# Keeping the bias of rows 0 to 127 on chip for six heads: a change to an attention and MLP kernel

## The chip, the cores and the metric

The kernel runs on one core of one Trainium2 chip. The metric is the device time of one execution in microseconds (us), the median of several runs.

## The reference

Attention with a bias that depends on the row i and the distance to column j, then a feed-forward block and a gated block, all in float32 on inputs of 4 batches, 8 heads, 576 rows, head width 64. Only the first part matters here:

```
def _attn_ref(q, k, v, w1, b1, w2):
    scores = scale * np.matmul(q, k.transpose(0, 1, 3, 2))
    pos = np.arange(S)
    rel = (pos[:, None] - pos[None, :]).astype(np.float32)
    x = (np.log1p(np.abs(rel)) / np.log1p(np.maximum(pos[:, None], 1.0)))[..., None]
    h = np.maximum(x @ w1 + b1, 0.0)          # 32 hidden units
    bias = h @ w2                             # 576 x 576 x 8 heads
    scores = scores + bias.transpose(2, 0, 1)[None]
    ...
```

A softmax over each row and the product with v follow; then a LayerNorm with a relu MLP and a residual; then a gated MLP and a residual.

## The kernel before, in words

**Bias stage (the first 53 us or so).** The 576 rows of the bias are made in 36 groups of 16 rows, numbered z, in the order `ORDER` (line 58): 16 to 23, 8 to 15, 0 to 7, 24 to 35. The place in that order is y, so that z = 0 is y = 16 and z = 7 is y = 23. For a group, `units` (L324) makes four tiles m (relu of a shifted log row) on ScalarE or VectorE as the table `WHO` says (L333, L335); `sums` (L338) multiplies them by w2 on TensorE into PSUM tiles pt (L347), from a pool of six; `finish` (L380) evacuates pt, scaled, into an SBUF tile o, its columns to the right and to the left of the diagonal apart, each by ScalarE (L354) or VectorE (L356) as the table `EV` says, and stores that tile. Partition 8r + h of o holds row r of the group for head h, 591 columns wide, so one tile holds all eight heads of 16 rows. The pool of m has 14 buffers, that of o (`bs`) has 10. Each loop step y issues the m tiles of y + 2, then the sums of y, then `finish` of y - 1, so each engine's order is fixed by this loop.

**The way through DRAM.** `store` (L358, the issue is L368) writes o to a scratch tensor scr in DRAM, which turns eight heads on partitions into rows on partitions when it is read back. Groups with z < FULL = 24 store all of o at once (295.5 KB), on the SP queue. Groups 24 to 35 go into three wider tiles of four groups each (the pool `aspare`, 4*591 columns); in the bias stage only heads 0 and 1 of them are stored, in two pieces for each four groups (`GROUPS`: three groups at once, 110.8 KB for a head, then the fourth, 36.9 KB; the last ones for head 1 are issued by ScalarE). The other six heads follow with a store of the whole tile (1182 KB), put into a list `held` and issued at the attention slots `HELD` = 2, 3 and 9.

**Reading back.** `read(k)` (L370) loads bias rows 128k to 128k + 127 of heads 0 and 1 (L376 for odd k; two loads for even k, L262 and L263, which turn the columns; L276 for the last 64 rows). The table `READ` says behind which y each is issued on the SP queue. The other six heads are loaded pair by pair, during the attention of the pair ahead (`load_bias`, from slot 19 on for the first of them), into two buffers `bias` that alternate, of the pools `abias0` and `abias1`.

**What else the SP queue carries there.** The raw k, q and v of the first two units (L216, L210), and `place_q` (L236), which moves halves of q between partitions.

**Attention (about 53 to 315 us).** 16 units (head pair, batch), each of 9 slots of 64 or 128 rows; a hand-written list (`FIRST` for unit 0, `SEQ` for the others) gives the order of steps: `S n` are the score products on TensorE (L708), `add n` adds the bias and takes the row minimum on VectorE (`ct`, L714), `exp n` is on ScalarE (L728), `T n` are transposes (L734). `emit_slot` (L880) issues the held stores and, for later units, the loads of q, k and v; GpSimd splits them into high and low parts (L114, L120). The two MLP blocks follow to the end.

**Completion of transfers.** The built program gives each DMA the next of eight completion semaphores, DMAHW0 to DMAHW7, in turn, and a DMA's issue first waits until the semaphore's last user has landed. An instruction that must wait for a DMA waits for its semaphore.

Of the kernel before, what the change touches and what calls it, by code (L numbers as in the profile page):

```python
# [9 lines left out]
F32 = mybir.dt.float32  # L10
# [8 lines left out]
B, H, S, D, DM = 4, 8, 576, 64, 512  # L19
# [57 lines left out]
    AA AA AA AA AA AA AA AA AD DD AA DA  # L77
""".split()

READ = {20: [2], 27: [0], 29: [1], 32: [3], 35: [4]}  # L80

FULL = 24
GROUPS = ((3, 2), (1, 3))
HELD = (2, 3, 9)
QK = 5, 16, 11, 22
GATE = 35
STAGES = 8
# [8 lines left out]
def mark(label):  # L96
    pass
# [3 lines left out]
def block_kernel(  # L101
# [8 lines left out]
    def new_pool(name, bufs, stack=None, **kw):  # L110
        return (stack or ctx).enter_context(tc.tile_pool(name=name, bufs=bufs, reuse_waits="tile", **kw))
# [82 lines left out]
    bp1 = new_pool("abias1", 1, left)  # L194
    raw, ops, bias, M = {}, {}, {}, {}
# [4 lines left out]
    M["held_at"] = right.enter_context(ExitStack())  # L200
    M["spare"] = new_pool("aspare", (36 - FULL) // 4, M["held_at"], side="right")
    Qb = [qp.tile([128, 2 * S + 64], F32R, name=f"q{j}") for j in range(2)]
# [4 lines left out]
    def load_q(u, pool_=rawp):  # L207
        hp, b = UNITS[u]
        t = raw.setdefault(u, {})["q"] = pool_.tile([128, 2, S], F32R, name="q")
        sp.dma_start(out=t[:, 1].bitcast(F32), in_=a["q"][b, hp])  # L210
# [20 lines left out]
    def place_q(u):  # L231

        t, Q = raw[u].pop("q"), Qb[u % 2]
        for h in range(2):
            for z in range(2):
                sp.dma_start(out=Q[64 * z:64 * z + 64, q_of(h)].bitcast(F32), in_=t[64 * h:64 * h + 64, z].bitcast(F32))  # L236
# [15 lines left out]
    def new_bias(hp):  # L252
        bias[hp] = (bp0, bp1)[hp % 2].tile([128, 9, S], F32, name="bias")
# [11 lines left out]
    def load_bias(hp, z):  # L265

        if hp not in bias:
            new_bias(hp)
        if z < 2:
            t = bias[hp][:, 5 * z:5 * z + 4]  # L270
            src = rows(2 * hp, 0, 512)[:, z].rearrange("(n p) j -> p n j", p=128)
            turned(t[:, ::2], src[:, ::2])
            sp.dma_start(out=t[:, 1::2], in_=src[:, 1::2])
        else:
            for h in range(2):
                sp.dma_start(out=bias[hp][64 * h:64 * h + 64, 4], in_=rows(2 * hp, 512, 64)[:, h])  # L276
# [4 lines left out]
    with ExitStack() as c:  # L281
# [32 lines left out]
        )  # L314
        pool.memset(mhalf, -0.5)
        new_bias(0)
        for t in Qb:
            pool.memset(t[:, S:S + 64].bitcast(F32), 0.0)
        def reach(z):

            l, r = 16 * z + 15, S - 16 * z
            return l, r, max(l + 1, r)
# [28 lines left out]
        def scaled(who, z, o, i):  # L351
            f = scl[:, z:z + 1]
            if who == "A":
                act.activation(o, i, AF.Copy, scale=f)  # L354
            else:
                dve.tensor_scalar(out=o, in0=i, scalar1=f, scalar2=None, op0=ALU.mult)  # L356

        def store(z, n, src, heads=None):  # L358

            f = 16 + 16 * z * H * PITCH - reach(z)[0]  # L360
            if heads is None:
                dims, src = [[PITCH, 128]], src
            else:
                f += heads * PITCH
                dims, src = [[H * PITCH, 16]], src[heads::H]
            dims += [[16 * (H * PITCH - 1), n], [1, 591]]
            q = act if heads == 1 and z + n > 34 else sp
            q.dma_start(out=bass.AP(scr.tensor, scr.offset + f, dims), in_=src.rearrange("p (s j) -> p s j", s=n))  # L368

        def read(k):  # L370
            if k == 4:
                load_bias(0, 2)
                return
            t, src = bias[0][:, k::5], rows(0, 128 * k, 128)
            if k % 2:
                sp.dma_start(out=t, in_=src)  # L376
            else:
                turned(t, src)

        def finish(z, pts):  # L380
            l, r, n = reach(z)
            if z < FULL:
                t = stg.tile([128, 591], F32, name="o")
            else:
                if z % 4 == 0:
                    spare[z // 4] = M["spare"].tile([128, 4 * 591], F32, name="o")
                t = spare[z // 4][:, 591 * (z % 4):][:, :591]
            left, right = t[:, :l + 1][:, ::-1], t[:, l:]
            for o, pt in pts:
                scaled(EV[ORDER.index(z)][0], z, (right if z < 18 else left)[:, o], pt)  # L390
            if z < 18:
                scaled(EV[ORDER.index(z)][1], z, left[:, 1:], pts[0][1][:, 1:l + 1])
            else:
                scaled(EV[ORDER.index(z)][1], z, right[:, 1:], pts[0][1][:, 1:r])
            if z < FULL:
                store(z, 1, t)
            else:

                for n, at in GROUPS:
                    if z % 4 == at:  # L400
                        for h in range(2):
                            store(z + 1 - n, n, spare[z // 4][:, 591 * (at + 1 - n):591 * (at + 1)], h)
                if z % 4 == 3:
                    M.setdefault("held", []).append(lambda: store(z - 3, 4, spare[z // 4]))
            for k in READ.get(ORDER.index(z), ()):
                read(k)

        spare = {}
# [3 lines left out]
        for y, z in enumerate(ORDER):  # L412
# [5 lines left out]
            if y >= BEHIND:  # L418
                finish(*late.pop(0))
# [12 lines left out]
            if y == QK[2]:  # L432

                KH, KL = (qkp.tile([128, 2, S + 64], F32R, name=n) for n in ("kh", "kl"))
                k = raw[0].pop("k")
# [9 lines left out]
                split_v(0)  # L445
        while late:
            finish(*late.pop(0))


    tiles = [[4 * b + j for j in range(4)] for b in range(B)] + [[16, 17]]  # L450
# [95 lines left out]
    side = {}  # L546
# [6 lines left out]
    def conv_first(rcp):  # L553

        at = [(0, 1)] + [(u, j) for u in range(1, 12) for j in range(2)]

        def put(p, f):
            conv_at.setdefault(p, []).append(f)

        for z in range(4):  # L560

            def load_piece(z=z):
                r = rcp.tile([128, 1024], I32, name="r")
                if z < 2:
                    sp.dma_start(out=r.rearrange("p (k f) -> p k f", k=2), in_=w1v[:, 2 * z:2 * z + 2, :512])
                else:
                    sp.dma_start(out=r, in_=w2v[:, z - 2])
                return r

            ld, stages, w = convert(rcp, 512, load_piece)  # L570
            i = 5 * z + 3
            put(at[i - 2], ld)
            for q, f in enumerate(stages[:5]):
                put(at[min(i + q, 22)], f)
            last = at[min(i + 4, 22)][0], 2
            put(last, stages[5])
            put(last, lambda z=z, w=w: sp.dma_start(out=wc0[z // 2, :, 512 * (z % 2):512 * (z % 2) + 512], in_=w()))
# [81 lines left out]
    with ExitStack() as c:  # L659
# [220 lines left out]
        def emit_slot(u, n):  # L880

            mark(f"att {u}.{n}")
            k = 9 * u + n
            PT[:] = PA[(k + 1) % 2], PA[k % 2]
            hp, b = UNITS[u]
            if n == 0 and u + 1 < NU:
                place_q(u + 1)
            if n == 1 and "last" in M:
                M.pop("last")()
            if n == 5 and u + 2 < NU:  # L890
                load_q(u + 2)
                load_k(u + 2)
            for f in side.pop(k - 1, []) + ([M["held"].pop(0)] if k in HELD else []):
                f()
            if k == HELD[-1]:
                M["held_at"].close()
                conv_first(new_pool("arc", 2, M["rc"]))
            if u == 12 and n == 0:
                open_first()
            if hp < 3 and b == 2 and n in (1, 4, 7):  # L900
                load_bias(hp + 1, n // 3)

        emit = dict(
            slot=emit_slot, sq=emit_sq, kh=emit_kh, vh=emit_vh, C=emit_C, cp=lambda u: emit_C(u, 2), S=emit_S, add=emit_add, exp=emit_exp, T=emit_T, hi=emit_hi, lo=emit_lo, RT=emit_RT, RThi=emit_RThi,
            RTlo=emit_RTlo, PV=emit_PV, Pev=emit_Pev, O=emit_O, Oev=emit_Oev, fo=emit_fo, fx=emit_fx, Or=emit_Or, oc=emit_oc, ra=emit_ra, rb=emit_rb, xr=emit_xr,
        )
# [511 lines left out]
def build(tc, nc, aps, out):  # L1418
    a = {n: (p.bitcast(I32) if n in ("moe_w_ch1", "moe_w_ch2", "moe2_w_in", "moe2_w_out") else p) for n, p in aps.items()}
    with tc.manual_schedule():  # L1420
        block_kernel(tc, nc, a, out)
# [18 lines left out]
```

## Time and profile before

| | |
|---|---|
| median of 3 runs | 946.3 us (946.25 to 948.57) |
| the profiled execution | 945.16 us; span of its records 943.4 us |
| TensorE busy | 922.5 us, 98% of the span |
| VectorE busy | 720.6 us, 76% |
| ScalarE busy | 494.9 us, 52% |
| GpSimd busy | 425.1 us, 45% |
| granted TensorE clock | full speed (9 of 9 tenths shown) in all 40 slices of the page |

Shares are averages over stages with different limits. Busy time is what an engine spent on instructions; a time in brackets behind a row is the idle time of the engine ahead of it, with what ended it. "L354" is line 354 of the kernel. SPq and ACTq are the queues on which SP and ScalarE issue DMAs. A DMA's landing is counted from its issue.

### The profile page before, as it was taken

The numbers are of one execution on the slowest core, as the hardware profiler recorded it, in microseconds if no ns is written. First come the engines' busy times: TensorE is split into PE (matmuls) and PEld (weight loads), VectorE is DVE, ScalarE is ACT, GpSimd is POOL, SyncE is SP. The second block draws the span as 40 slices with busy tenths as digits, with TensorE's granted clock in tenths as the row PEclk, the third lists the DMA queues.
The fourth block names the chain that finished last, engine by engine and source line by source line (L and its number), as shares of the span: only waits on it lengthen the run. The fifth ranks groups of instructions, "written<-read, shape, count | busy, mean of one in ns | idle before, by whom it ended". The sixth has DMA issues, their size and how long they took to land.

```text
span 943.4 us, 16015 instructions
## 1 busy us (share of the span) xinstructions
PE 922.5 (98%) x5681; PEld 805.8 (85%) x5681; DVE 720.6 (76%) x1433; ACT 494.9 (52%) x1108; POOL 425.1 (45%) x555
## 2 busy tenths in 40 slices
PE   7889999999999999999999999999999999999998
PEld 2269999999999888888888888888888998989996
DVE  7988999999889687885779798979765656455452
ACT  8979999999998754322222222223132635253340
POOL 0068788978999543332224333433300524133251
PEclk9999999999999999999999999999999999999999
DMA  6878847757563561212122333233222000001001
GB/s 230 283 234 258 270 137 214 236 162 226 158 206 85 177 196 31 70 33 89 61 68 92 123 99 122 88 124 99 101 67 104 23 1 23 24 0 58 1 34 67
DMA packets 57983, 110.23 MB, mean 117 GB/s; under 512 B 10032, under 2 KB 21040, under 8 KB 57648
## 3 DMA queue, kind: packets, MB, share of 16 engines
q1 hardware_dynamic: 57504, 108.64, 36.1%
q8 instruction: 45, 0.74, 0.3%
q10 hardware_dynamic: 400, 0.58, 0.2%
q14 instruction: 34, 0.28, 0.1%
HBM read 71.37 MB, written 28.38 MB: 106 GB/s over the span
## 4 chain that ended last, share of the span: by engine, by line
PE 91%; DVE 5%; POOL 1%; DMA 1%; issue 1%; ACT 1%; DVEq 0%; SPq 0%; POOLq 0%; ACTq 0%
PE psh L124 21%; PE psy L124 21%; PE psa L124 10%; PE s L708 8%; PE PB L797 8%; PE psa L1284 6%; PE pt L734 6%; PE psa L1266 5%; DVE m L335 4%; PE pt L487 1%; PE OB L803 1%; PE s L744 1%; PE pt L347 1%; DVE ct L714 0%; DMA L<-in_c_log_dram 0%
## 5 line engine op out<-in xcount | busy, mean ns | idle before, releaser
L124 PE MATMUL psh<-blk,w1h 128*128 128x512 f32 (+1 forms) x640 | 151.5, 368 | 0.0
L176 POOL TENSOR_TENSOR cvl<-cvl,cvt 128x512 f32<-128x512 f32 x44 | 56.9, 1293 | 206.6 <-DVE cvt L173 179.0
L655 ACT ACTIVATE hh<-psh 128x512 fp32r<-128x512 f32 (+1 forms) x80 | 44.1, 553 | 194.4 <-PE psh L124 193.2
L124 PEld LDWEIGHTS psh<-blk,w1h 128*128 128x128 f32 x640 | 113.3, 188 | 20.8 <-DVE blk L120 0.2
L714 DVE CUSTOM_DVE_ANT_0 ct<-s,bias 128x576 f32<-128x576 f32 x144 | 107.0, 752 | 16.6 <-PE s L708 7.1
L728 ACT ACTIVATE a<-ct,sm 128x576 f32<-128x576 f32 x144 | 112.2, 779 | 3.2 <-DVE sm L714 2.6
L1087 DVE TENSOR_TENSOR x_sb<-psy,x_sb 128x512 f32<-128x512 f32 x144 | 97.2, 683 | 9.1 <-PE psy L124 8.6
L656 DVE SCALAR_TENSOR_TENSOR hl<-psh,hh 128x512 fp32r<-128x512 f32 (+1 forms) x80 | 50.5, 632 | 56.5 <-ACT hh L655 56.5
L124 PE MATMUL psy<-w2h,hh 128*128 128x512 f32 x288 | 90.2, 394 | 0.1
L124 PE MATMUL psy<-w2l,hh 128*128 128x512 f32 x288 | 88.9, 390 | 0.0
L124 PE MATMUL psy<-w2h,hl 128*128 128x512 f32 x288 | 88.8, 389 | 0.0
L734 PE MATMUL pt<-ident,a 128*128 128x128 f32 x576 | 84.9, 273 | 0.3 <-DVE at0l L120 0.3
L124 PE MATMUL psh<-blk,w1l 128*128 128x512 f32 (+1 forms) x320 | 79.0, 368 | 0.0
L708 PE MATMUL s<-kh,q 128*128 128x288 f32 x320 | 72.0, 314 | 3.1 <-DVE sm L714 2.4
L734 PEld LDWEIGHTS pt<-ident,a 128*128 128x128 f32 x576 | 68.6, 141 | 1.1 <-DVE at0l L120 0.6
L708 PE MATMUL s<-kl,q 128*128 128x288 f32 x320 | 65.8, 295 | 0.0
L124 PEld LDWEIGHTS psh<-blk,w1l 128*128 128x128 f32 x320 | 56.8, 189 | 10.0
L124 PEld LDWEIGHTS psy<-w2l,hh 128*128 128x128 f32 x288 | 54.0, 188 | 11.5
L124 PEld LDWEIGHTS psy<-w2h,hl 128*128 128x128 f32 x288 | 54.0, 188 | 11.5
L177 POOL TENSOR_TENSOR cvw<-cvl,cvw 128x512 f32<-128x512 f32 x44 | 59.9, 1362 | 3.5
L124 PEld LDWEIGHTS psy<-w2h,hh 128*128 128x128 f32 x288 | 52.6, 188 | 9.9 <-issue 0.2
L120 DVE TENSOR_TENSOR at0l<-pt,at0h 128x512 fp32r<-128x512 f32 (+1 forms) x80 | 49.5, 619 | 5.6 <-ACT at0h L117 5.2
(202 smaller groups left out, 2173.5 us busy)
## 6 DMA issues: line engine op xcount, KB each, us to landing
r<-in_moe_w_ch_dram SPq DMA_DIRECT2D x32, 512.0 KB, 4.8
k<-in_k_dram SPq DMA_DIRECT2D x16, 640.0 KB, 5.4
q<-q SPq DMA_DIRECT2D x64, 144.0 KB, 2.7
scr<-o SPq DMA_DIRECT2D x24, 295.5 KB, 3.3
v<-in_v_dram SPq DMA_DIRECT2D x16, 384.0 KB, 3.5
q<-in_q_dram SPq DMA_DIRECT2D x16, 288.0 KB, 3.7
bias<-scr SPq DMA_DIRECT2D x8, 576.0 KB, 5.7
bias<-scr SPq DMA_DIRECT2D x8, 512.0 KB, 5.0
```

Of the source, the lines that this page charges most:

```text
L120: (eng or dve).tensor_tensor(out=o, in0=i, in1=hi.bitcast(F32), op=ALU.subtract)
L124: pe.matmul(ps, lhsT=w, rhs=x, start=start and j == 0, stop=stop and j == len(terms) - 1)
L176: pool.tensor_tensor(out=T["l"], in0=T["l"], in1=T["t"].bitcast(F32), op=ALU.mult)
L177: pool.tensor_tensor(out=T["w"], in0=T["l"], in1=T["w"], op=ALU.add)
L656: dve.scalar_tensor_tensor(out=hl[:, f, :n], in0=ps[:, :n], scalar=0.0, in1=hh[:, f, :n].bitcast(F32), op0=ALU.max, op1=ALU.subtract)
L708: pe.matmul(s[:, x, :288], lhsT=w, rhs=m[:, 288 * x:288 * x + 288], start=j == 0, stop=j == len(prs) - 1)
L714: dve.tensor_tensor_reduce(out=ct, in0=s[:, :, :288], in1=bias[UNITS[u][0]][:, n].rearrange("p (a b) -> p a b", a=2), scale=-0.125, scalar ...
L728: act.activation(weights(n), ct.rearrange("p a b -> p (a b)"), AF.Exp, scale=-1.0, bias=mt, accum_out=SU[u % 2][:, n:n + 1])
L734: pe.transpose(PA[k % 2][:, j], e[:, 128 * j:128 * j + 128], ident)
L797: pe.matmul(d, lhsT=w, rhs=m, start=q == 0, stop=q == len(terms) - 1)
L1087: dve.tensor_tensor(out=x_sb[:, t], in0=ps, in1=x_sb[:, t], op=ALU.add)
L1284: pe.matmul(ps[:, z, :288], lhsT=v, rhs=w[:, 288 * z:288 * z + 288], start=(q == 0), stop=(q == len(terms) - 1))
```

## The change

Rows 0 to 127 (z = 0 to 7) are treated as rows 384 to 575 are: their groups are evacuated into a tile that stays in SBUF, only heads 0 and 1 are stored in the bias stage, in pieces of three groups and one, and the whole tiles (four groups, 1182 KB each) are stored at two more attention slots, 11 and 13, both in the second unit. The tile `early` is two-dimensional, 9*576 columns wide, and is the first buffer of the pool `abias1`, which nothing else uses before slot 19. The 591 columns of a group lie in it one after the other. The spare pool is released at the third held store, as before. `READ` issues the reads behind other groups: rows 256 to 383 behind y = 18 (was 20), rows 128 to 255 behind y = 22 (was 29), rows 384 to 511 behind y = 33 (was 32). Nothing is computed otherwise, and the tables `WHO`, `TURN` and `EV` are the same.

```
--- before.py
+++ after.py
@@ -77,11 +77,17 @@
     AA AA AA AA AA AA AA AA AD DD AA DA
 """.split()
 
-READ = {20: [2], 27: [0], 29: [1], 32: [3], 35: [4]}
+READ = {18: [2], 22: [1], 27: [0], 33: [3], 35: [4]}
 
 FULL = 24
+
+
+def kept(z):
+    return z < 8 or z >= FULL
+
+
 GROUPS = ((3, 2), (1, 3))
-HELD = (2, 3, 9)
+HELD = (2, 3, 9, 11, 13)
 QK = 5, 16, 11, 22
 GATE = 35
 STAGES = 8
@@ -314,6 +320,7 @@
         )
         pool.memset(mhalf, -0.5)
         new_bias(0)
+        early = bp1.tile([128, 9 * S], F32, name="bias")
         for t in Qb:
             pool.memset(t[:, S:S + 64].bitcast(F32), 0.0)
         def reach(z):
@@ -379,10 +386,13 @@
 
         def finish(z, pts):
             l, r, n = reach(z)
-            if z < FULL:
+            if not kept(z):
                 t = stg.tile([128, 591], F32, name="o")
             else:
-                if z % 4 == 0:
+                if z % 4 == 0 and z < 8:
+
+                    spare[z // 4] = early[:, 591 * z:591 * z + 4 * 591]
+                elif z % 4 == 0:
                     spare[z // 4] = M["spare"].tile([128, 4 * 591], F32, name="o")
                 t = spare[z // 4][:, 591 * (z % 4):][:, :591]
             left, right = t[:, :l + 1][:, ::-1], t[:, l:]
@@ -392,7 +402,7 @@
                 scaled(EV[ORDER.index(z)][1], z, left[:, 1:], pts[0][1][:, 1:l + 1])
             else:
                 scaled(EV[ORDER.index(z)][1], z, right[:, 1:], pts[0][1][:, 1:r])
-            if z < FULL:
+            if not kept(z):
                 store(z, 1, t)
             else:
 
@@ -401,7 +411,7 @@
                         for h in range(2):
                             store(z + 1 - n, n, spare[z // 4][:, 591 * (at + 1 - n):591 * (at + 1)], h)
                 if z % 4 == 3:
-                    M.setdefault("held", []).append(lambda: store(z - 3, 4, spare[z // 4]))
+                    M.setdefault("held", []).append((z < 8, z, lambda: store(z - 3, 4, spare[z // 4])))
             for k in READ.get(ORDER.index(z), ()):
                 read(k)
 
@@ -445,6 +455,7 @@
                 split_v(0)
         while late:
             finish(*late.pop(0))
+        M["held"].sort(key=lambda x: x[:2])
 
 
     tiles = [[4 * b + j for j in range(4)] for b in range(B)] + [[16, 17]]
@@ -890,9 +901,9 @@
             if n == 5 and u + 2 < NU:
                 load_q(u + 2)
                 load_k(u + 2)
-            for f in side.pop(k - 1, []) + ([M["held"].pop(0)] if k in HELD else []):
+            for f in side.pop(k - 1, []) + ([M["held"].pop(0)[2]] if k in HELD else []):
                 f()
-            if k == HELD[-1]:
+            if k == HELD[2]:
                 M["held_at"].close()
                 conv_first(new_pool("arc", 2, M["rc"]))
             if u == 12 and n == 0:
```

The instructions of TensorE, VectorE, ScalarE and GpSimd stand in the same order as before; what moves is the SP queue, and what the engines wait for. In the program's order a row names the line, the operation, out<-in and the shape; in brackets stand the semaphores that it waits for (PE_49, DVE_49 and Activation_49 are those of the engines; `small` holds the scales). ScalarE's line 354 is line 361 of the changed kernel, SP's line 368 is 375, and `bias` as an output there is the tile `early`.

SP's queue from the store of group 0 on (y = 16), before: eight stores of whole groups, one for each z, with the loads of v and of rows 256 to 383 between them.

```order
L368 DMA scr<-o 128x591 [waits DMAHW5_49,DVE_49,Activation_49]
L216 DMA v<-in_v_dram 128x768 [waits DMAHW6_49]
L368 DMA scr<-o 128x591 [waits DMAHW7_49,DVE_49,Activation_49]
L368 DMA scr<-o 128x591 [waits DMAHW0_49,Activation_49]
L368 DMA scr<-o 128x591 [waits DMAHW1_49,Activation_49]
L368 DMA scr<-o 128x591 [waits DMAHW2_49,Activation_49]
L262 DMA bias<-scr 128x2x512 [waits DMAHW3_49]
L263 DMA bias<-scr 128x2x64 [waits DMAHW4_49]
L368 DMA scr<-o 128x591 [waits DMAHW5_49,Activation_49]
L368 DMA scr<-o 128x591 [waits DMAHW6_49,DVE_49]
L368 DMA scr<-o 128x591 [waits DMAHW7_49,Activation_49]
```

The same stretch in the change: one load of v, then pairs of small stores, head 0 and head 1, for groups 0 to 2, 3, 4 to 6 and 7, and two reads.

```order
L222 DMA v<-in_v_dram 128x768 [waits DMAHW5_49]
L375 DMA scr<-bias 16x3x591 [waits DMAHW6_49,DVE_49,Activation_49]
L375 DMA scr<-bias 16x3x591 [waits DMAHW7_49]
L268 DMA bias<-scr 128x2x512 [waits DMAHW0_49]
L269 DMA bias<-scr 128x2x64 [waits DMAHW1_49]
L375 DMA scr<-bias 16x591 [waits DMAHW2_49,Activation_49]
L375 DMA scr<-bias 16x591 [waits DMAHW3_49]
L375 DMA scr<-bias 16x3x591 [waits DMAHW4_49,DVE_49]
L375 DMA scr<-bias 16x3x591 [waits DMAHW5_49]
L383 DMA bias<-scr 128x2x576 [waits DMAHW6_49]
L375 DMA scr<-bias 16x591 [waits DMAHW7_49,Activation_49]
L375 DMA scr<-bias 16x591 [waits DMAHW0_49]
```

The stores of groups 0 to 2 use DMAHW6 and DMAHW7, those of groups 4 to 6 DMAHW4 and DMAHW5. The next two places are ScalarE's evacuations of group 3 and of group 7. Of group 2's end and group 3's (the 128x264 rows are the two right halves of group 3), before:

```order
L354 ACTIVATE o<-pt,small 128x272 [waits PE_49]
L354 ACTIVATE o<-pt,small 128x47
L354 ACTIVATE o<-pt,small 128x264 [waits DMAHW0_49,PE_49]
L354 ACTIVATE o<-pt,small 128x264 [waits PE_49]
L354 ACTIVATE o<-pt,small 128x63
```

DMAHW0 is here the store of the group ten places ahead, whose buffer o takes. In the change the same row waits for DMAHW6 and DMAHW7, with values that the two stores of groups 0 to 2 bring when they have landed:

```order
L361 ACTIVATE bias<-pt,small 128x272 [waits PE_49]
L361 ACTIVATE bias<-pt,small 128x47
L361 ACTIVATE bias<-pt,small 128x264 [waits DMAHW7_49,DMAHW6_49,PE_49]
L361 ACTIVATE bias<-pt,small 128x264 [waits PE_49]
L361 ACTIVATE bias<-pt,small 128x63
```

ScalarE's evacuation of group 7 (128x464), twelve rows on, differs likewise: it waited for DMAHW4, the store of an older user of its buffer, and waits in the change for DMAHW4 and DMAHW5 with the values of the two stores of groups 4 to 6.

The evacuations of groups 27, 31 and 35, which follow stores of their tile's first three groups in the same way, wait for PE_49 alone in both programs.

The third place is SP's queue at the read of rows 384 to 511, before. The stores of groups 31 and 32 to 34 lie around it; the store of head 1 of groups 32 to 34 is issued by ScalarE.

```order
L368 DMA scr<-o 16x591 [waits DMAHW3_49,Activation_49]
L368 DMA scr<-o 16x591 [waits DMAHW4_49]
L376 DMA bias<-scr 128x2x576 [waits DMAHW3_49,DMAHW4_49,DMAHW2_49,DMAHW5_49,DMAHW1_49,DMAHW0_49]
L368 DMA scr<-o 16x3x591 [waits DMAHW6_49,DVE_49,Activation_49]
L368 DMA scr<-o 16x591 [waits DMAHW7_49,DVE_49,Activation_49]
```

The same rows in the change:

```order
L375 DMA scr<-o 16x591 [waits DMAHW3_49,Activation_49]
L375 DMA scr<-o 16x591 [waits DMAHW4_49]
L383 DMA bias<-scr 128x2x576 [waits DMAHW4_49,DMAHW5_49,DMAHW3_49,DMAHW7_49,DMAHW2_49,DMAHW1_49]
L375 DMA scr<-o 16x3x591 [waits DMAHW6_49,DVE_49,Activation_49]
L375 DMA scr<-o 16x591 [waits DVE_49,Activation_49]
```

The read waits for another six of the eight semaphores; its place among the stores is the same.

## Rows read from the trace of the kernel before

**Rows 1.** Busy times by stage: us, PE, PEld, DVE, ACT, POOL, PEclk, DMA, GB/s.

```profile
10.00:52.00 42.00, 33.27 (x328) 9.27 (x327) 41.20 (x114) 39.67 (x90) 1.01 (x2) 1.00 0.83 282
75.00:315.00 240.00, 239.43 (x1931) 237.95 (x1930) 218.37 (x559) 224.62 (x596) 209.26 (x258) 1.00 0.63 187
```

**Rows 2.** The chain that ended last, its transfers at the seam: start us, us, what.

```profile
52.09 2.31 DMA scr<-o
...
54.48 3.96 DMA bias<-scr
```

**Rows 3.** Timeline of VectorE at the seam: start us, us, what, [idle before <-releaser].

```profile
56.61 0.69 DVE L120 TENSOR_TENSOR at0l<-pt,at0h 128x512 fp32r<-128x512 f32 x1 [0.20 <-ACT at0h L117]
58.60 0.76 DVE L714 CUSTOM_DVE_ANT_0 ct<-s,bias 128x576 f32<-128x576 f32 x1 [1.29 <-DMA bias<-scr]
```

**Rows 4.** Timeline of ScalarE around groups 2, 3, 6 and 7.

```profile
30.56 0.68 ACT L354 ACTIVATE o<-pt,small 128x272 f32<-128x272 f32 x2
31.12 0.49 ACT L354 ACTIVATE o<-pt,small 128x264 f32<-128x264 f32 x1
...
32.65 0.91 ACT L354 ACTIVATE o<-pt,small 128x512 f32<-128x512 f32 x2 [0.37 <-PE pt L347]
33.88 0.91 ACT L354 ACTIVATE o<-pt,small 128x496 f32<-128x496 f32 x2 [0.32 <-PE pt L347]
...
35.85 0.64 ACT L354 ACTIVATE o<-pt,small 128x480 f32<-128x480 f32 x1
...
37.32 0.89 ACT L354 ACTIVATE o<-pt,small 128x464 f32<-128x464 f32 x2
```

**Rows 5.** Timeline of SP's queue there (issues).

```profile
28.06 2.67 SPq L236 DMA_DIRECT2D q<-q  x4
30.84 0.52 SPq L368 DMA_DIRECT2D scr<-o  x1
31.41 0.88 SPq L216 DMA_DIRECT2D v<-in_v_dram  x1
```

**Rows 6.** DMA issues at 30.5 and 31.8 (q, v): KB each, us to landing.

```profile
q<-q SPq DMA_DIRECT2D x1, 144.0 KB, 5.5
v<-in_v_dram SPq DMA_DIRECT2D x1, 384.0 KB, 5.7
```

**Rows 7.** Busy times, columns as in rows 1, of two stretches.

```profile
36.00:43.00 7.00, 6.38 (x54) 1.35 (x50) 7.00 (x21) 6.73 (x16) 0.00 (x0) 1.00 1.04 387
43.00:46.00 3.00, 1.83 (x20) 0.23 (x14) 3.00 (x9) 3.00 (x8) 0.00 (x0) 1.00 0.44 131
```

**Rows 8.** DMA issues at 43.3 and 49.8: the small stores of groups 24 to 35.

```profile
scr<-o SPq DMA_DIRECT2D x1, 110.8 KB, 2.4
scr<-o SPq DMA_DIRECT2D x1, 36.9 KB, 3.8
```

**Rows 9.** Timeline, VectorE's left halves of groups 6 and 32, ScalarE between and after.

```profile
37.95 0.32 DVE L356 TENSOR_SCALAR o<-pt,small 128x111 f32<-128x111 f32 x1
47.06 0.76 ACT L333 ACTIVATE m<-L,shift 128x560 f32<-128x560 f32 x1 [0.33 <-PE pt L347]
49.17 0.47 ACT L354 ACTIVATE o<-pt,small 128x264 f32<-128x264 f32 x1
50.75 0.27 DVE L356 TENSOR_SCALAR o<-pt,small 128x63 f32<-128x63 f32 x1
```

**Rows 10.** DMA issues at 62.9, 63.7 and 79.7: held stores, then a q.

```profile
scr<-o SPq DMA_DIRECT2D x1, 1182.0 KB, 5.4
scr<-o SPq DMA_DIRECT2D x1, 1182.0 KB, 8.6
q<-in_q_dram SPq DMA_DIRECT2D x1, 288.0 KB, 6.0
```

**Rows 11.** Timeline, GpSimd's splits for a unit, and TensorE's first use of them.

```profile
90.57 1.62 POOL L120 TENSOR_TENSOR kl<-k,kh 128x640 fp32r<-128x640 f32 x1
98.99 0.38 PE L708 MATMUL s<-kh,q 128*128 128x288 f32 x1
```

More of the change, by code (lines that the diff above doesn't have):

```diff
@@ L78, with kept @@
 """.split()
-READ = {20: [2], 27: [0], 29: [1], 32: [3], 35: [4]}
+READ = {18: [2], 22: [1], 27: [0], 33: [3], 35: [4]}
 FULL = 24
+def kept(z):
+    return z < 8 or z >= FULL
 GROUPS = ((3, 2), (1, 3))
-HELD = (2, 3, 9)
+HELD = (2, 3, 9, 11, 13)
 QK = 5, 16, 11, 22
@@ L316, in block_kernel @@
         new_bias(0)
+        early = bp1.tile([128, 9 * S], F32, name="bias")
         for t in Qb:
@@ L381, in finish @@
             l, r, n = reach(z)
-            if z < FULL:
+            if not kept(z):
                 t = stg.tile([128, 591], F32, name="o")
             else:
-                if z % 4 == 0:
+                if z % 4 == 0 and z < 8:
+                    spare[z // 4] = early[:, 591 * z:591 * z + 4 * 591]
+                elif z % 4 == 0:
                     spare[z // 4] = M["spare"].tile([128, 4 * 591], F32, name="o")
@@ L394, in finish @@
                 scaled(EV[ORDER.index(z)][1], z, right[:, 1:], pts[0][1][:, 1:r])
-            if z < FULL:
+            if not kept(z):
                 store(z, 1, t)
@@ L403, in finish @@
                 if z % 4 == 3:
-                    M.setdefault("held", []).append(lambda: store(z - 3, 4, spare[z // 4]))
+                    M.setdefault("held", []).append((z < 8, z, lambda: store(z - 3, 4, spare[z // 4])))
             for k in READ.get(ORDER.index(z), ()):
@@ L447, in block_kernel @@
             finish(*late.pop(0))
+        M["held"].sort(key=lambda x: x[:2])
     tiles = [[4 * b + j for j in range(4)] for b in range(B)] + [[16, 17]]
@@ L892, in emit_slot @@
                 load_k(u + 2)
-            for f in side.pop(k - 1, []) + ([M["held"].pop(0)] if k in HELD else []):
+            for f in side.pop(k - 1, []) + ([M["held"].pop(0)[2]] if k in HELD else []):
                 f()
-            if k == HELD[-1]:
+            if k == HELD[2]:
                 M["held_at"].close()
```

## The prediction

> **What bounds the kernel now.** I read first the busy times by stage, to see which engine sets the pace where. In the bias stage VectorE works 41.20 of 42.00 us and ScalarE 39.67, TensorE only 33.27; in attention TensorE works 239.43 of 240.00 us [rows 1]. So nothing that makes TensorE start later is made up behind the seam, and nothing off VectorE's and ScalarE's path in the bias stage counts. The whole kernel's share of 98% for TensorE hides this.
>
> Next the chain that ended last, at the seam: behind VectorE's last evacuations come a store that ScalarE issued at 52.09 (head 1 of groups 32 to 34) and a read of bias at 54.48, which is `read(3)`, rows 384 to 511 [rows 2]. VectorE's timeline shows the toll: it is free at 56.61 + 0.69 = 57.30 and waits until 58.60 for bias, 1.29 us, to begin `add 3` [rows 3]. That instruction is my yardstick. What moves it moves the end.
>
> The reader should see here that `read(3)` needs nothing of groups 32 to 34. What it waited for is that store's landing at 52.09 + 2.31 = 54.40 [rows 2], as one of the semaphores it waits on was that store's too. In the change it waits for another six semaphores (SP's order above), and no store of ScalarE's queue is among their users by then.
>
> **The change, part by part.** Durations are of the profiled execution, 945.16 us; the median, 946.3, lies 1.14 higher, and I add that at the end.
>
> *First the instructions.* TensorE, VectorE, ScalarE and GpSimd issue the same instructions of the same shapes in the same order: no cost. SP exchanges eight stores for eight small ones and later two whole ones.
>
> *The wait of group 3.* ScalarE's first evacuation of group 3 now stands behind the landing of both stores of groups 0 to 2 (ScalarE's order above). Before, it began at 31.12, straight behind group 2's, which end at 30.56 + 0.68 = 31.24, less their overlap [rows 4]. The stores cannot issue before group 2 is done, say 31.7 and 32.3. When do they land? No row shows a small store there, so I bound it. The queue is backlogged: the fourth q, issued at about 28.06 + 3/4 x 2.67 = 30.06 [rows 5], takes 5.5 us and lands at 35.5; v, issued at 31.41 [rows 5], takes 5.7 and lands at 37.1 [rows 6]. In these 1.6 us the queue moved v and one whole store, 679.5 KB, so 2.36 us for 1000 KB. In the change that whole store is gone: v lands at 35.5 + 0.9 = 36.4, and two stores of 110.8 KB follow at 0.26 each, to 36.9. So group 3 starts at 36.95, 5.8 late. The other bound is an idle queue: the store at 43.3 landed after 2.4 us [rows 8], when the share of the queue had fallen from 1.04 to 0.44 [rows 7]. From 32.1 that is 34.5, 3.4 us late. I take 5.8, since the row on the same DMAs in the same microseconds is the nearer one.
>
> The Trainium skill has a rule that would put the price at the other end: DMA: Bandwidth & Descriptors, section "Anatomy of one DMA — SWDGE (gpsimd) path", gives a fixed 2.0 us and the bytes by 436 GB/s, an estimate of 2.3 us for such a store. By that the first wait would be 3.3 us, and the trace's 5.5 us for 144 KB [rows 6] says that it leaves out what stands ahead in the queue.
>
> *The wait of group 7.* From group 3's start to the end of group 6's, before, 35.85 + 0.64 - 31.12 = 5.37 us went by, 0.37 + 0.32 of them idle for pt [rows 4], which is ready when ScalarE comes late: 4.68. So group 6 ends at 41.6. VectorE's left half of it, 0.32 us [rows 9], ends at 42.0. Then head 0 is stored, 0.6 later head 1, and by now the queue is empty, as the whole stores of groups 3 to 7 are gone: 2.4 us [rows 8], landed at 45.05. Group 7 starts at 45.1 where it was 37.32 [rows 4]: ScalarE is 7.8 late. If these stores take 3.8, as the slowest small row [rows 8], it is 9.2.
>
> *What is queued behind.* ScalarE's own m tiles, on which TensorE's sums wait. Of the 7.8 ScalarE gets back one idle time, 0.33 at 47.06 [rows 9]: 7.45 at group 32, whose first part ended at 49.17 + 0.47 = 49.64 [rows 9] and now ends at 57.1. Meanwhile VectorE runs ahead only as far as 14 buffers of m go. VectorE's left half of group 32 waits for that part, and goes from 50.75 [rows 9] to 57.15: 6.4 late. Behind it VectorE's path is as before, so it is free for `add 3` at 57.30 + 6.4 = 63.7.
>
> *The reads.* `read(2)` and `read(1)` come earlier, and their rows were not awaited. `read(3)`: group 31's evacuation ends before the row at 49.17 begins, so by 49.17 + 7.45 = 56.6 at the latest in the change; two small stores, the second issued 0.6 later, land 2.4 after that, at 59.6, and the read takes 3.96 [rows 2]: 63.6, just ahead of VectorE. So the 1.29 us of wait goes. With 3.8 for that store the wait would still be 1.3 [rows 8].
>
> *Two more held stores* in unit 1, beside TensorE. Their own issue costs SP 0.6 each. One landed after 5.4, the next, issued 0.6 later, after 8.6 [rows 10], so each fills the queue for 3.8 us. They lie ahead of the load of q for unit 3, which lands 6.0 after its issue at 79.57 now [rows 10]; at worst it is 7.6 late. Slot 11 is three slots ahead of it, 3 x 240/144 = 5.0 us, in which the queue, busy to 0.63 [rows 1], drains 0.37 x 5.0 = 1.9: 5.7 late. GpSimd's split ended at 90.57 + 1.62 = 92.2, and TensorE wants it at 98.99 [rows 11]: 6.8 us of slack cover 5.7. If the cover is gone, TensorE loses up to 2.
>
> **Sum.** `add 3` goes from 58.60 to 63.7: +5.1. That is 950.3 for the profiled execution, and with 1.14 a median of **951.4**.
>
> **The rivals.**
> - *The small stores land as on an idle queue.* Group 3 starts at 34.5, group 7 at 42.6 (the same 8.1 later as above), 5.3 late, less 0.33: 5.0 at group 32, whose first part ends at 54.6, so VectorE is 3.9 late: `add 3` at 57.30 + 3.9 = 61.2, +2.6, so **948.9**. Against it stand the 5.5 and 5.7 us [rows 6]. 0.12.
> - *Attention does stall*: GpSimd's late q reaches TensorE, or the slow last store keeps `read(3)` late. +1.3 to 2 on top: **953.4**. 0.15.
> - *TensorE's clock falls.* The trace shows 1.00 throughout [rows 1], with TensorE never long without work; two stalls of 5.8 and 3.4 us, of which it works through what the six PSUM tiles hold, are new. At the lower level (1.2 of 2.4 GHz) its share of 6.38 of 7.00 [rows 7] would double in the 4.68 us between them: at most +3.8, by half **953.4**. The Trainium skill, TensorE: Matmul & The Clock Gate, section "Why this matters for your kernels", advises against idle gaps between bursts of matmuls because the lower clock returns; no row here shows it. 0.10.
> - *The other side: not slower.* ScalarE's two waits cost nothing, because the program's values are those of long-landed users, as DMAHW0 to DMAHW4 were before. Then only `read(3)` counts: 1.29 less, **945.0**. The place is the row at 31.12 [rows 4]; it decides if the stores of groups 0 to 2 land by then, and they cannot issue before group 2 ends at 31.24. 0.06.
>
> **How the numbers follow.** 951.4 has 0.57. A measurement of this kernel tells about 0.3% from no change, 2.8 us here: 943.5 and 949.1 are the limits. Faster than 943.5: no case, 0.02 for what I have not seen. The same: the not-slower case, 0.06, and most of the idle queue's, 0.08, some of the first: 0.16. Slower: 0.82. The range reaches from just under the idle queue's 948.9 to the price of both late cases, 948.2 to 954.6: outside lie the not-slower case and a sum of two mishaps.
>
> **What would show it.** In the profile after: ScalarE's row of 128x264 near 36.95 with about 5.8 us idle ended by a DMA, the row of 128x464 near 45.1 with about 3.5; VectorE's 128x63 near 57.15; `add 3` near 63.7 with no idle time ended by DMA; the clock 1.00; attention as long as before. Wrong it is if these two rows show no wait, if VectorE's left halves are less late than ScalarE by more than 1 us, or if idle time turns up on TensorE behind 75 us.

## The result and the profile after

The changed kernel takes 954.0 us (median of 4 runs, 952.05 to 954.52) where the kernel before, beside it, takes 946.73: a ratio of 1.0072, 95% interval 1.0057 to 1.0086. It is slower, by 7.3 us where 5.1 were forecast, and lies in the range. The profiled execution took 954.52 us, its span 952.4; it is the slowest of the four, and the profiled execution before (945.16) was a quick one, so the two profiles lie 9.4 us apart.

First the busy times by stage of the changed kernel, with the columns of [rows 1], in the stretches of the two waits and in attention:

```profile
36.00:43.00 7.00, 3.58 (x21) 0.96 (x21) 2.28 (x7) 3.07 (x9) 0.00 (x0) 0.83 0.59 171
43.00:46.00 3.00, 1.89 (x12) 0.33 (x12) 1.60 (x5) 1.91 (x4) 0.00 (x0) 0.82 0.02 5
51.00:56.00 5.00, 4.81 (x32) 1.15 (x32) 3.24 (x9) 5.00 (x13) 0.00 (x0) 0.67 0.21 59
75.00:315.00 240.00, 239.48 (x1927) 237.84 (x1925) 217.19 (x561) 223.65 (x595) 203.04 (x249) 1.00 0.68 208
```

From 36 to 43 us VectorE and ScalarE, which had no idle time to speak of there [rows 7], work 2.28 and 3.07 of 7 us. From 43 to 46 the DMA engines stand still too (share 0.02): the stores of groups 4 to 6 issue only at 44.77 and 45.37, behind VectorE's left half of group 6. The granted clock fell. In attention TensorE is as full as before [rows 1].

ScalarE's timeline shows the two waits, at the places where [rows 4] show none:

```profile
30.81 1.15 ACT L361 ACTIVATE bias<-pt,small 128x272 f32<-128x272 f32 x3
39.93 1.05 ACT L361 ACTIVATE bias<-pt,small 128x264 f32<-128x264 f32 x3 [7.97 <-DMA scr<-bias]
47.74 0.90 ACT L361 ACTIVATE bias<-pt,small 128x464 f32<-128x464 f32 x2 [2.83 <-DMA scr<-bias]
```

Group 2's evacuations end at 31.96; then ScalarE stands 7.97 us until the stores of groups 0 to 2 have landed, and before group 7 it stands again, 2.83 us. What was in front of these stores the DMA issues show (the fourth q at 31.61, the two stores at 32.96 and 33.61, one of groups 4 to 6, one of group 31):

```profile
q<-q SPq DMA_DIRECT2D x1, 144.0 KB, 6.6
...
scr<-bias SPq DMA_DIRECT2D x1, 110.8 KB, 6.6
...
scr<-bias SPq DMA_DIRECT2D x1, 110.8 KB, 6.2
...
scr<-bias SPq DMA_DIRECT2D x1, 110.8 KB, 2.3
...
scr<-o SPq DMA_DIRECT2D x1, 36.9 KB, 3.3
```

A small store lands 6.2 to 6.6 us after its issue where the q's and v stand ahead of it, and 2.3 where nothing does. For DMAs that GpSimd issues, the Trainium skill (DMA: Bandwidth & Descriptors, section "Anatomy of one DMA — SWDGE (gpsimd) path") gives a fixed 2.0 us and the bytes by 436 GB/s, an estimate of 2.3 us for 110.8 KB. The 2.3 us of SP's store with nothing ahead of it agrees; the 6.2 and 6.6 us don't, since that sum has no term for what stands ahead.

VectorE's timeline, to be set beside [rows 9] and [rows 3]:

```profile
44.40 0.33 DVE L363 TENSOR_SCALAR bias<-pt,small 128x111 f32<-128x111 f32 x1 [6.12 <-ACT bias L361]
52.98 1.28 DVE L342 TENSOR_SCALAR m<-L,shift 128x512 f32<-128x512 f32 x3 [1.49 <-PE pt L354]
59.66 2.12 DVE L363 TENSOR_SCALAR o<-pt,small 128x63 f32<-128x63 f32 x6 [0.43 <-ACT o L361]
66.89 0.76 DVE L725 CUSTOM_DVE_ANT_0 ct<-s,bias 128x576 f32<-128x576 f32 x1 [0.64 <-DMA bias<-scr]
```

Group 6's left half is 6.5 late, group 32's 8.9, and `add 3` starts at 66.89 instead of 58.60: 8.3 late. Is that all? VectorE's last `ct` of attention, before and after:

```profile
309.37 0.75 DVE L714 CUSTOM_DVE_ANT_0 ct<-s,bias 128x576 f32<-128x576 f32 x1
```

```profile
317.71 0.75 DVE L725 CUSTOM_DVE_ANT_0 ct<-s,bias 128x576 f32<-128x576 f32 x1
```

8.34 apart: 139 such instructions later the distance is what it was at `add 3`. The two more held stores in unit 1 cost attention nothing. The rest of the 9.0 us between the two spans lies behind these rows, where the change alters nothing (633.99 us before, 634.70 after; 633.99 to 635.87 over all the profiled executions).

### The profile page after: what moved, and what is told of

It reads as the page before. It is cut to its first block, busy times and chain, and to the rows that moved or that the text cites. A ratio compares the mean times of both kernels' runs of the same rounds, so it can differ in the third digit from the quotient of the medians.

```text
span 952.4 us, 16005 instructions
## 1 busy us (share of the span) xinstructions
PE 929.1 (98%) x5681; PEld 808.3 (85%) x5681; DVE 719.5 (76%) x1433; ACT 494.3 (52%) x1108; POOL 424.4 (45%) x555
## 5 line engine op out<-in xcount | busy, mean ns | idle before, releaser
L130 PEld LDWEIGHTS psy<-w2h,hh 128*128 128x128 f32 x288 | 52.4, 188 | 10.4 <-DVE x_sb L1098 0.7
```

The costliest lines, as they stand in the source:

```text
L130: pe.matmul(ps, lhsT=w, rhs=x, start=start and j == 0, stop=stop and j == len(terms) - 1)
```

## The experiments

Theory: the two waits of ScalarE are the whole cost. Rivals: the moved reads, the two more held stores, the clock. Ratios are to the kernel before on the same chip.

**e1_pitch: the waits taken away.** The program of the change waits although groups 0 to 2 and group 3 lie in different columns, and groups 27, 31 and 35 don't wait in the same position. Their tiles are 4 times 591 columns wide; `early` is 9 times 576. In the program with `early` 8 x 591 columns wide both waits are gone.

```
-        early = bp1.tile([128, 9 * S], F32, name="bias")
+        early = bp1.tile([128, 8 * 591], F32, name="bias")
```

> The change with the tile early 8*591 columns wide in place of 9*576, nothing else. In the built program ScalarE's evacuations of groups 3 and 7 then wait for TensorE alone. Theory (the two waits on the stores' landings are the cost): no idle time ended by a DMA on ScalarE there, clock 1.00 through the bias stage, add 3 near 57.5, time 945.0, between 944.2 and 946.5, so about 9 less than the change. Rival (the two more held stores delay attention, or the moved reads cost something): still 1 to 3 slower than before, 947 to 949. Rival (the wait goes elsewhere, to another user of the small stores' semaphores): above 950, with a new idle time on ScalarE or VectorE ended by a DMA.

Measured: 951.65 us, ratio 1.0051 (1.0037 to 1.0065). A little less than the change (the two intervals overlap), and 6.6 us more than the 945.0 expected. ScalarE's timeline at groups 3 and 7 and at its late store, with SP's queue and VectorE's `add 3` behind it:

```profile
30.13 1.06 ACT L361 ACTIVATE bias<-pt,small 128x272 f32<-128x272 f32 x3
37.27 0.89 ACT L361 ACTIVATE bias<-pt,small 128x464 f32<-128x464 f32 x2
...
52.02 0.65 ACTq L375 DMA_DIRECT2D scr<-o  x1
```

```profile
45.41 0.47 SPq L269 DMA_DIRECT2D bias<-scr  x1
54.38 2.48 SPq L375 DMA_DIRECT2D scr<-o  x4
58.39 0.37 SPq L383 DMA_DIRECT2D bias<-scr  x1
```

```profile
62.60 0.76 DVE L725 CUSTOM_DVE_ANT_0 ct<-s,bias 128x576 f32<-128x576 f32 x1 [5.34 <-DMA bias<-scr]
```

The waits on ScalarE are gone, group 7 is at 37.27 (37.32 before), and the bias stage is as before. But `add 3` waits 5.34 us for `read(3)`. SP issued nothing from 45.88 to 54.38: the next store, of groups 28 to 30, waits for DMAHW1, which ScalarE's store of 52.02 holds until it lands at 54.32. The program gave that late store its semaphore ahead of an earlier one on SP. That is the last rival of the expectation, a wait that went elsewhere. In the kernel before the same kind of wait was the 1.29 us of [rows 3].

**e2_reads: the reads alone**, in the kernel before (the table READ of the change).

> The kernel before with the table READ of the change alone. Theory: the reads are off the path but for rows 384 to 511, whose wait of 1.29 us at add 3 may go: 945.0 to 946.7. Rival (the order of the reads carries the loss): above 948.

Measured: 947.14, ratio 1.0003 (0.9994 to 1.0013). No difference: the moved reads cost nothing that can be told. Its `read(3)` still waited for ScalarE's store (landed at 55.72, `read(3)` issued at 55.80), and `add 3` waited 1.33, so the 1.29 us did not go.

**e3_one_wait: the wait of group 7 taken away.**

```
-                for n, at in GROUPS:
+                for n, at in (((4, 3),) if 4 <= z < 8 else GROUPS):
```

> The change with groups 4 to 7 stored in one piece for a head, behind group 7, so that no evacuation follows a store of its part of the tile: the wait of group 3 stays, that of group 7 goes. Theory: ScalarE still waits about 8 us at group 3 and no longer at group 7 (2.83 in the profile of the change), some of which was given back before: 951.5 to 952.5. Rival (the two waits do not add, the first sets all): 954.0.

Measured: 952.8, ratio 1.0059 (1.0044 to 1.0074). Its `read(3)` shares a semaphore with ScalarE's store again:

```profile
62.96 0.76 DVE L725 CUSTOM_DVE_ANT_0 ct<-s,bias 128x576 f32<-128x576 f32 x1 [1.39 <-DMA bias<-scr]
```

So neither this run nor e1_pitch gives a wait's price by itself. The second set of runs removes the sharing.

**e4_clock: TensorE kept busy in the waits** (16 more matmuls on the zero tile).

```
+            busy({24: 7, 26: 5, 27: 4}.get(y, 0))
```

> The change with 7, 5 and 4 more matmuls on the zero tile ahead of the sums of y = 24, 26 and 27, to fill TensorE's idle time in the two waits. Granted clock there 0.83, 0.82 and 0.67 in the change; here near 1.00. Theory (the clock that fell costs on top of the waits): ScalarE's waits as long as before, VectorE's idle time of 1.49 on pt at 52.98 gone, 952.0 to 952.7. Rival (the clock costs nothing, as the waits set the pace): 954.0, or later by what the added matmuls hold up.

Measured: 955.46, ratio 1.0084 (1.0068 to 1.0100), so no gain. Its busy times by stage, and its timelines of ScalarE at group 3 and VectorE at group 32 and `add 3`:

```profile
36.00:43.00 7.00, 5.08 (x32) 2.16 (x32) 2.47 (x8) 4.44 (x12) 0.00 (x0) 1.00 0.47 161
43.00:46.00 3.00, 3.00 (x19) 1.41 (x16) 2.95 (x9) 0.55 (x2) 0.00 (x0) 1.00 0.35 81
51.00:56.00 5.00, 4.48 (x57) 1.76 (x51) 5.00 (x13) 5.00 (x13) 0.00 (x0) 1.00 0.37 81
```

```profile
38.56 1.06 ACT L361 ACTIVATE bias<-pt,small 128x264 f32<-128x264 f32 x3 [6.89 <-DMA scr<-bias]
```

```profile
58.31 2.12 DVE L363 TENSOR_SCALAR o<-pt,small 128x63 f32<-128x63 f32 x6 [1.59 <-ACT o L361]
65.45 0.76 DVE L726 CUSTOM_DVE_ANT_0 ct<-s,bias 128x576 f32<-128x576 f32 x1 [0.54 <-DMA bias<-scr]
```

The clock stayed at 1.00 through both waits. From the start of group 3 to `add 3` it took 65.45 - 38.56 = 26.89 us, of which 0.54 is the wait for `read(3)`: 26.35. In the change, at 0.83, 0.82 and 0.67, it took 66.89 - 39.93 = 26.96, less 0.64: 26.32. VectorE waits less for pt, and in its place 1.59 us for ScalarE at group 32, where the change has 0.43. So in the bias stage the lower clock cost nothing, since ScalarE, late by the waits, set the pace.

Behind `add 3` it did cost. This execution reached `add 3` 1.44 us ahead of the change's and its last `ct` of attention (317.98) 0.27 behind: 1.71 lost. Of these 0.35 came at `add 4`, with a read that was late, and 0.8 where the clock fell here, to 0.50 from 73 to 75 us: the `ct` of 77.85 came 3.08 us after the one ahead of it (74.77), and in the change, at 1.00 there, 2.28 (75.86 to 78.14). That is why the shorter wait of this execution brought no shorter time; the last 0.5 I have not traced.

**The second set: no semaphore shared with ScalarE.** In all four below, SP issues every store:

```
-            q = act if heads == 1 and z + n > 34 else sp
+            q = sp
```

*f1_pitch_sp: e1_pitch so.*

> e1_pitch with all stores issued by SP. In e1_pitch SP stood from 45.9 to 54.33 with the store of groups 28 to 30, waiting for the landing of ScalarE's store of 52.02, whose completion semaphore it shares; read(3) came 6 us late and add 3 waited 5.34. Theory (that shared semaphore is what ate the gain of e1_pitch): the stores of groups 28 to 30 issue near 46.7, read(3) near 53, add 3 starts at 57.3 without waiting for a DMA; 945.0 to 946.0, so 6 less than e1_pitch. Rival (something else of the change costs 5, the reads' places or the two held stores): 950 or more, with add 3 near 57.5 and the loss behind it.

Measured: 945.48, ratio 0.9983 (0.9971 to 0.9996); run again, 945.05, 0.9971 (0.9959 to 0.9984):

> f1_pitch_sp again, beside the three below on one chip: 945 to 946, 0.1 to 0.3% less than before.

SP's queue and VectorE of f1_pitch_sp:

```profile
47.20 3.03 SPq L375 DMA_DIRECT2D scr<-o  x4
51.66 0.36 SPq L383 DMA_DIRECT2D bias<-scr  x1
```

```profile
57.68 0.75 DVE L725 CUSTOM_DVE_ANT_0 ct<-s,bias 128x576 f32<-128x576 f32 x1
```

The stores of groups 28 to 30 issue at 47.20, `read(3)` at 51.66, and `add 3` waits for nothing. It is faster than both kernels: 0.2 to 0.3% less than before.

*f2_before_sp: the kernel before so.*

> The kernel before with all stores issued by SP. read(3) then waits for the landing of group 31's stores (53.36) and not for ScalarE's of 52.09 (54.40): theory, 1.0 less at add 3, 945.3 to 946.3. Rival (the stores of the last groups come later on SP and rows 512 to 575 late for add 4): same as before or up to 1 more.

Measured: 946.82, ratio 0.9994 (0.9983 to 1.0006), no difference that can be told. `read(3)` issued at 55.46, now for group 31's store, which stood behind `read(0)` and `read(1)` in the queue; `add 3` waited 0.57 and `add 4` 0.62. The rival came out.

*f3_after_sp and f4_one_wait_sp: the change so, and the change with group 3's wait alone.*

> The change with all stores issued by SP. In the change no row of SP ahead of read(3) waits for ScalarE's stores, so the theory of the two waits on ScalarE expects no change: 953 to 954.5. Rival (the shared semaphores cost in the change as well): below 951.

> e3_one_wait with all stores issued by SP: the wait of group 3 alone, 6.28 us in e3_one_wait's profile, and no shared semaphore (there read(3) waited for ScalarE's store, 1.39 at add 3). Theory: 1.4 less than e3_one_wait, 951.0 to 951.8; the wait of group 7 in the change is then worth the difference to f3_after_sp, 2 to 3. Rival (read(3) waits as long for group 31's store): 952.8.

Measured: 955.68, ratio 1.0094 (1.0075 to 1.0114), 1.2 us above what was expected, and 951.38, 1.0055 (1.0034 to 1.0075), from runs that spread from 949.03 to 958.03. The timelines of ScalarE at groups 2 and 3 and of VectorE at `add 3`, first of f3_after_sp, then of f4_one_wait_sp, and ScalarE's at group 2 of f1_pitch_sp:

```profile
31.21 1.16 ACT L361 ACTIVATE bias<-pt,small 128x272 f32<-128x272 f32 x3
38.95 1.05 ACT L361 ACTIVATE bias<-pt,small 128x264 f32<-128x264 f32 x3 [6.59 <-DMA scr<-bias]
```

```profile
65.99 0.76 DVE L725 CUSTOM_DVE_ANT_0 ct<-s,bias 128x576 f32<-128x576 f32 x1 [0.73 <-DMA bias<-scr]
```

```profile
30.18 1.05 ACT L361 ACTIVATE bias<-pt,small 128x272 f32<-128x272 f32 x3
37.33 1.05 ACT L361 ACTIVATE bias<-pt,small 128x264 f32<-128x264 f32 x3 [6.09 <-DMA scr<-bias]
```

```profile
61.43 0.76 DVE L725 CUSTOM_DVE_ANT_0 ct<-s,bias 128x576 f32<-128x576 f32 x1 [0.24 <-PE s L755]
```

```profile
30.85 2.10 ACT L361 ACTIVATE bias<-pt,small 128x272 f32<-128x272 f32 x6
```

The three executions came to group 2 at different times, so I count from there. With no wait, one and two, `add 3` follows group 2's start by 26.83, 31.25 and 34.78 us. The first wait costs 4.4 us, where ScalarE stood 6.09: part of it is given back, as from group 3 to group 7 ScalarE then takes 4.83 us where f1_pitch_sp takes 5.99. In the other 3.5 is a first wait that was 0.5 longer in f3_after_sp. From group 3 on, behind the first wait, the two take 24.10 and 27.04 us, or 23.86 and 26.31 without `add 3`'s own wait, so the second wait costs 2.5 to 2.9, where ScalarE stood 2.83: about what it lasts. The medians (945.48, 951.38, 955.68) put it at 4.3, those of e3_one_wait and the change (952.8, 954.0) at 1.2; the runs spread too far to price one wait.

*h1_one_column: f1_pitch_sp with one column more.*

```
-        early = bp1.tile([128, 8 * 591], F32, name="bias")
+        early = bp1.tile([128, 8 * 591 + 1], F32, name="bias")
```

> f1_pitch_sp with the tile early one column wider, 8*591 + 1. In the built program both waits of ScalarE are back. Theory (the width decides, as the tile's pieces are told apart only where a group's 591 columns divide it): first wait 6 to 7 us, second 2.8, time 954 to 956, about 9 to 10 more than f1_pitch_sp. Rival (the waits cost less when ScalarE issues no stores, and f3_after_sp was slow for its larger tile): below 950.

Measured: 953.37, ratio 1.0059 (1.0044 to 1.0074), with

```profile
39.60 1.06 ACT L361 ACTIVATE bias<-pt,small 128x264 f32<-128x264 f32 x3 [6.76 <-DMA scr<-bias]
```

One unused column costs 8 us (953.37 against 945.05, on the same chip). The total is a little under the expected 954; the first wait, and the second with 2.83, are as expected.

*g2_before_sp_reads and g3_pitch_sp_oldreads: which part of f1_pitch_sp makes its gain.* The kernel before with SP's stores and the reads of the change; and f1_pitch_sp with the reads of before.

> The kernel before with all stores issued by SP and the table READ of the change: what f1_pitch_sp has, but for the rows kept on chip. In f2_before_sp read(3) waited until 55.30 for group 31's stores, which stood in the queue behind read(0) and read(1). Theory A (the gain of f1_pitch_sp is the freed read(3), and the kept rows add nothing): add 3 without a wait for a DMA, 945.2 to 946.0, as f1_pitch_sp. Theory B (it needs the eight whole stores gone from the queue): read(3) still late, 946.5 to 947.3, as f2_before_sp.

> f1_pitch_sp with the table READ of the kernel before: rows 128 to 255 are read ahead of the stores of groups 28 to 31 again. Theory A (the reads' places make the gain): add 3 waits 0.5 to 1 for read(3), 946.3 to 947. Theory B (the kept rows make it): no wait, 945.2 to 946.0.

Measured: 947.46, ratio 1.0002 (0.9991 to 1.0012), and 947.19, 0.9997 (0.9987 to 1.0007): neither gains. VectorE's `add 3` and `add 4` (the last 64 rows), of g2_before_sp_reads and of g3_pitch_sp_oldreads:

```profile
57.46 0.76 DVE L714 CUSTOM_DVE_ANT_0 ct<-s,bias 128x576 f32<-128x576 f32 x1 [0.19 <-DMA bias<-scr]
...
61.96 0.76 DVE L714 CUSTOM_DVE_ANT_0 ct<-s,bias 128x576 f32<-128x576 f32 x1 [0.49 <-DMA bias<-scr]
```

```profile
58.09 0.76 DVE L725 CUSTOM_DVE_ANT_0 ct<-s,bias 128x576 f32<-128x576 f32 x1 [0.94 <-PE pt L745]
...
62.95 0.76 DVE L725 CUSTOM_DVE_ANT_0 ct<-s,bias 128x576 f32<-128x576 f32 x1 [0.85 <-DMA bias<-scr]
```

In the first `read(3)` issued at 53.19, 2.0 later than in g1_again (51.17), as whole stores are still in the queue; 0.19 of it shows at `add 3`, and the next read is late at `add 4`. In the second both are later still (its row at `add 3` names PE, but `read(3)` landed at 57.93, 0.16 ahead of it, as far ahead as the read in g2_before_sp_reads, 57.30). My expectations looked at `add 3` alone: Theory B's late read came out in g2 and Theory A's in g3, both with times 0.2 above their ranges.

But the larger part of the loss comes later. These are two `ct` of unit 0, of g1_again and then of g2_before_sp_reads:

```profile
66.38 0.75 DVE L725 CUSTOM_DVE_ANT_0 ct<-s,bias 128x576 f32<-128x576 f32 x1
...
68.66 0.76 DVE L725 CUSTOM_DVE_ANT_0 ct<-s,bias 128x576 f32<-128x576 f32 x1 [0.86 <-PE s L755]
```

```profile
66.94 0.75 DVE L714 CUSTOM_DVE_ANT_0 ct<-s,bias 128x576 f32<-128x576 f32 x1
...
70.45 0.76 DVE L714 CUSTOM_DVE_ANT_0 ct<-s,bias 128x576 f32<-128x576 f32 x1 [1.51 <-PE s L744]
```

The first takes 2.28 us at a granted clock of 1.00, the second 3.51 at 0.50 (66 to 68 us); in g3_pitch_sp_oldreads it is 3.53, at 0.50 from 67 to 69. So the late reads cost about 0.4 and 0.8 at `add 4`, and the fall of the clock behind them 1.2 more, as TensorE sets the pace there. In f2_before_sp and h1_one_column the clock falls to 0.50 as well, a little earlier among these rows, and they lose 0.1 by it. That the late reads made the clock fall is likely and not shown. The gain needs all three edits: rows kept without the waits, early reads, and no shared semaphore.

## Why the prediction was right, and where its terms were off

*The mechanism* was right: two waits of ScalarE on landings of small stores, read from the built order, on a path with no slack. f1_pitch_sp and h1_one_column show it: one unused column, and with it the two waits, separates 945 from 953.

*The first wait: mis-sized.* "Group 3 starts at 36.95, 5.8 late": it started at 39.93, 8.8 late. The steps behind the fourth q were right (v took 1.0 in the queue for 0.9, each store 0.3 for 0.26), but that q landed at 38.23 for 35.5, being issued 1.5 later and landing after 6.6 for 5.5 us. Five other executions that have this wait stood 6.09 to 6.89 us, so the profiled one, with 7.97, is at the upper end and the forecast, 5.7 from the end of group 2, under the lower. One traced landing was taken for the queue's depth. The idle queue's rival, 3.4, was refuted by the 6.2 and 6.6 us.

*The second wait* was forecast at "about 3.5" and stood 2.83.

*What is queued behind: right.* From group 3 to group 7 and to VectorE at group 32 the forecast went from 5.8 to 7.8 and 6.4 late; measured it was 8.8, 10.4 and 8.9. So the lateness grew by 0.1 where 0.6 was forecast: what was given back and what the second wait added are about as worked out, and the 2.5 that is missing at group 32 is the first wait's.

*The reads: half right.* The 1.29 us at `add 3` was to go; 0.64 stayed, since group 31's second store took 3.3 us for the assumed 2.4, and `read(3)` issued at 62.65. `read(0)` ahead of it had landed at 59.36, and from 59.4 to 61.7 the core's DMA engines moved only 34 GB/s; why, stays open. I had named the semaphore shared with ScalarE as what `read(3)` waited for before, and that was right (e2_reads still pays 1.33), but freeing `read(3)` alone was no gain: f2_before_sp and g2_before_sp_reads are as slow as before. The rival of 945.0, in which the waits cost nothing and the 1.29 goes, had its price right: f1_pitch_sp, in which both are so, takes 945.05 to 945.48. Wrong in it was that the waits of the change cost nothing.

*Attention: right.* The load of q for unit 3 was to be 5.7 us late and covered by 6.8 of slack. In the change GpSimd and TensorE show

```profile
100.90 0.84 POOL L120 TENSOR_SCALAR q<-q 128x576 fp32r<-128x576 f32 x1 [5.78 <-DMA q<-in_q_dram]
...
104.71 1.57 POOL L126 TENSOR_TENSOR kl<-k,kh 128x640 fp32r<-128x640 f32 x1
```

```profile
107.19 0.51 PE L719 MATMUL s<-kh,q 128*128 128x288 f32 x2
```

The q came at 100.90 where 86.90 + 8.3 = 95.2 would have been on time, 5.7 late; the split ended at 106.28, 0.9 ahead of TensorE's use.

*The clock.* The sign of a clock of 1.00 failed, and the rival, with 0.10, was right that it falls (0.83, 0.82, 0.67: 1.2 in place of 2.4 GHz for part of each stretch). It was wrong on the price in the bias stage: from group 3 to `add 3`, less the wait for `read(3)`, the change takes 26.32 us and e4_clock, at 1.00, 26.35. The advice of the Trainium skill (TensorE: Matmul & The Clock Gate, section "Why this matters for your kernels") is against idle gaps between bursts of matmuls. Here the fall of the clock agrees with it. What it costs depends on who sets the pace: nothing behind ScalarE's waits, 0.8 us in e4_clock and 1.2 in g2_before_sp_reads in attention.

*The time.* 2.2 us lie between the forecast of +5.1 and the +7.3 measured. In the profiled execution `add 3` is 8.3 late, of which 0.6 was there at group 2 already (30.81 for 30.19), ahead of the waits. From group 2's start to `add 3` it takes 36.08 us, and 34.35 to 34.82 in the three other executions with both waits, against 28.41 before: 5.9 to 6.4 later, and 7.7 in this one. So the forecast was 0.8 to 2.6 short, most of it by the first wait.

## What to carry to other kernels

Count a transfer that an evacuation waits for as the queue's depth at that moment, not as its own size, and look in the built order for waits that no data asks for: here a tile whose width its pieces did not divide, and a completion semaphore that a late store of another queue held. When a false wait is taken away, look again for the next: the first repair alone moved the loss from ScalarE's evacuations to SP's queue, and only the second, with the reads moved and the rows kept, paid. To price a wait, count inside each trace from a row ahead of it: the executions here come to the same row up to 2.3 us apart (group 2 at 30.02 to 32.30).

## What was not expected

- One column of a tile's width is worth 8 us: with 8 x 591 columns the program has no wait between groups of the same tile, with 8 x 591 + 1 it has. That pieces are told apart by rows of equal pitch is my reading of three widths (9 x 576 has the waits too) and of the tiles of 4 x 591, not shown.
- The completion semaphores are shared by the queues, and are not always given out in the order in which a queue's transfers can run: in e1_pitch SP issued nothing for 8.5 us (45.88 to 54.38), held by a store that ScalarE issued at 52.02. Some 7.7 of it had a store ready, as in g1_again the same store issues at 46.70.
- The same fall of the clock to half cost nothing in the bias stage and 0.8 to 1.2 us in attention, behind reads that were late by less than 1 us.
